# Attention and experts in one kernel: order of the read-back at a visit, places of key and factor products, second-weight splits in four parts

## The chip, the cores and the metric

The kernel runs on one core of one Trainium2 chip. The metric is the device time of one execution in microseconds (us); lower is better. In the texts PE is the matmul engine (TensorE), DVE is VectorE, ACT is ScalarE, POOL is GpSimd and SP is the engine whose queue issues most DMAs.

## What is computed

A polynomial-sketch attention over 4 batches, 4 heads, 1088 tokens and 32 columns a head, and behind it four experts, whose outputs are summed with normalized weights:

```python
def phi(x):
    a = np.einsum('rd,bhsd->bhsr', S1, x)
    b = np.einsum('rd,bhsd->bhsr', S2, x)
    return np.einsum('bhsi,bhsj->bhsij', a, b).reshape(*x.shape[:-1], r * r)
kv = np.einsum('bhsf,bhsd->bhfd', phi(k), v); z = np.sum(phi(k), axis=2)
attn = einsum(phi(q), kv) / (einsum(phi(q), z) + 1e-06)
x = attn.transpose(0, 2, 1, 3).reshape(4352, 128)
p = domain_probs / (domain_probs.sum(-1, keepdims=True) + 1e-09)
for e in range(4):
    out += p[:, e:e+1] * (np.maximum(x @ w1[e], 0.0) @ w2[e])
```

x has 4352 rows of 128; w1 is 128 x 1024 and w2 1024 x 128 for each of the four experts. All is float32.

## The kernel before, in words

**Chunks, experts, half-steps.** The 4352 rows of x are dealt into 11 chunks (`CHUNKS`, L95: 128, 448, 480, 480, six of 448, 128). A chunk m runs 16 steps: four for each expert e, and a step makes two blocks of 128 hidden rows, one in each half-step. "(m, e)" below is expert e of chunk m, and r0 to r7 are its eight half-steps. The half-steps are counted through the kernel; chunk m covers 32m to 32m+31. The lists `W2_AT` (L92), `KEYS_AT` (L814) and `UNITS_AT` (L820) give the half-steps at which side work is put into the stream: `first` (L1098) calls `work` once in each half-step, and `work` (L1408) runs what is due. `plan` entries (keys, units) are one higher than the count of `at_half` entries (w2 parts): 51 in `KEYS_AT` and 50 in `W2_AT` are the same half-step. Every engine executes its own instructions strictly in the order in which this program emits them.

**One half-step.** PE multiplies x by a block of w1 in three matmuls: two (L1147, L1148), then ACT scales the sum in PSUM (L1149), and one half-step later PE adds a third (L1199). ACT then takes the ReLU (L1203 for a block that is split, L1208 for one that is not). For a split block DVE makes the second part `hb` (L1175, in `lower`) and, once for two blocks, the third part `hd` (L1178). The second product (L1272, in `passed`) takes for a split block three matmuls, a, b and d, in PE's faster format (fp32r), and for a block that is not split one plain float32 matmul, "x", that is recorded as two. Six of eight blocks are split (`THREE`, L70); where (m, e) is in `MORE_IN` (L97), seven are. `DEAL` and `DEAL_MORE` (L75 to L83) say in which slot, counted in half-steps from r0, each second matmul is due: b1, which needs the second `hb`, at slot 4, x2 at slot 5, the last d6 and x7 at slot 11, which is r3 of the next expert. In chunk 1 the experts 0 and 1 are not split at all (`whole`).

**Accumulators.** PSUM has one bank `o0` (parts a and b) and one bank `o1` (parts d and x) for the second product. When an expert has ended, ACT copies `o0` (L1275) and DVE adds or copies `o1` out (L1304, L1301 in `gather`), POOL weights the result (L1311, L1313). The next expert's x2, or its d0 where there is no x2, cannot start before DVE has emptied `o1`.

**Attention and visits.** Attention runs beside the experts. Keys (`key_pieces`, L520) are turned, projected and multiplied: four `key_product` (L469, on DVE) for a batch. Queries come in units of 512 or 576 rows (`later`, L747). For a unit w: `unit_turn` transposes (DVE, L580), `unit_project` multiplies on PE, writes the factors to DRAM (L775), `unit_rows` (L779) reads them back as four tiles of factor rows (L786, L788, spread over 128 partitions), `unit_product` (L797) multiplies two pairs of them on DVE (L800), and the "visit" (L836) makes the attention output: PE multiplies, DVE divides (`attend_inverse`, `attend_scale`) and transposes. Then `attend_out` (L704), a generator, stores the tile to the DRAM buffer `xd` in four DMAs (L728) up to its first yield, and up to its second reads it back into `ring` in the layout of the experts (L739). At the end of the visit for w the factor rows of w+1 are read. All these DMAs are issued by SP, one after another. `token_parts` (L976) later splits a chunk of `ring` for the experts: ACT makes `xa` (L900), DVE `xb` and `xd` (L903), four steps ahead of the chunk.

**Second weights.** `second_weight_parts` (L918) splits the six blocks of w2[e] into three fp32r parts, in half-steps of chunk 1: ACT splits columns (L900), DVE joins (L903).

Of the kernel before, what the change touches and what calls it, by code (L numbers as in the profile page):

```python
# [24 lines left out]
def kernel(  # L25
# [65 lines left out]
    ]  # L91
    W2_AT = (36, 37, 38), (40, 41, 42), (44, 45, 46), (51, 52, 54)  # L92
    TOKENS_AT = 11, 12

    CHUNKS = [P, 448, 480, 480] + [448] * 6 + [P]  # L95
    NC = len(CHUNKS)
    MORE_IN = {(2, 2), (3, 2), (4, 2), (5, 1), (5, 2), (6, 2), (7, 0), (7, 1), (7, 2), (8, 0), (8, 1), (8, 2), (9, 0), (9, 1), (9, 2), (9, 3)}  # L97
    MORE_AT = {0: (100, 102), 1: (56, 57), 2: (38, 39), 3: (129, 131)}
    START = [sum(CHUNKS[:m]) for m in range(NC)]
    assert all(sum(u) == S for u in UNITS) and sum(CHUNKS) == B * S  # L100
# [79 lines left out]
    def more(m, e):  # L180
        return (m, e) in MORE_IN

# [361 lines left out]
    def key_sums(b):  # L544
        sums[b] = psum(ps_h, "h")
        for p in range(2):
            key_sum(b, p, sums[b])

    def key_end(b):

        key_blocks(b, sums.pop(b))
# [126 lines left out]
    def attend_inverse(nd, laid):  # L678

        tiles, banks = banks_of(laid)  # L680
        rc = apool.tile([P, XW // 32], F32, tag="rc", name="rc")
        for i, t0, t1 in banks:
            nc.vector.tensor_scalar(
                out=rc[:, H * t0 : H * t1],
                in0=_ap(nd[i], 0, P, D, [[D + 1, H * (t1 - t0)]]),
                scalar1=1e-6, scalar2=1.0, op0=ALU.add, op1=ALU.mult,
            )
        nc.vector.reciprocal(rc[:, 0 : H * tiles], rc[:, 0 : H * tiles])
        return rc

    def attend_scale(nd, laid, rc):

        xs = apool.tile([P, XW], F32, tag="qT", name="xs")
        banks = banks_of(laid)[1]
        for i, t0, t1 in banks:
            nc.vector.tensor_tensor(
                out=_ap(xs, 0, P, P * t0, [[D, H * (t1 - t0)], [1, D]]),
                in0=_ap(nd[i], 0, P, 0, [[D + 1, H * (t1 - t0)], [1, D]]),
                in1=_ap(rc, 0, P, H * t0, [[1, H * (t1 - t0)], [0, D]]),
                op=ALU.mult,  # L700
            )
        return xs
# [48 lines left out]
    def unit_turn(w):  # L751

        b, c, n, u = later[w]
        turned[w] = query_turn(b, c, n)
        if w and u == len(UNITS[b]) - 1 and b + 1 < B:
            load_rows(q, b + 1, "qn")

    def unit_project(w):

        b, c, n, u = later[w]  # L760
        qT, n2 = turned.pop(w), n // 2
        qc = psum(ps_h, "h")
        for i in range(2):
            for _ in range(2):
                on_side(
                    lambda s: qc[half[s], 0:n2],
                    lambda s: (sx if b else first_sx[0])[:, HP * i : HP * i + HP],
                    lambda s: qT[:, n2 * s : n2 * s + n2],
                    start=(i == 0),
                    stop=(i == 1),  # L770
                )
        qs = apool.tile([P, QW // 2], F32, tag="qf", name="qs")
        nc.scalar.copy(qs[:, 0:n2], qc[:, 0:n2])
        for s in range(2):
            nc.sync.dma_start(qd[b, u, :, n2 * s : n2 * s + n2], qs[half[s], 0:n2])  # L775
        if not w:
            load_rows(q, 1, "qn")
# [19 lines left out]
    def unit_product(w, p):  # L797

        n, (qp, qb) = later[w][2], factors[w]
        nc.vector.tensor_tensor(out=qp[p][:, 0:n], in0=qp[p][:, 0:n], in1=qb[p][:, 0:n], op=ALU.mult)  # L800

    def unit_visit(w):

        b, c, n, _ = later[w]
        products[w] = attend_products(b, c, n, factors.pop(w)[0])
# [3 lines left out]
    def add(hs, run):  # L809

        plan.setdefault(hs, []).append(run)

    FIRST_AT = (1, 2, 4, 5, 7, 9, 10, 12, 14, 15, 15, 15, 17, 18, 18, 19, 21, 23, 23)
    KEYS_AT = {  # L814
# [3 lines left out]
    }  # L818

    UNITS_AT = (  # L820
        (30, 43, 44, 47), (41, 73, 75, 79), (70, 103, 106, 111), (102, 134, 137, 143), (132, 157, 161, 175),
        (165, 191, 196, 207), (200, 214, 217, 222),
    )

    def lay_plan():

        of_first = queries(0, P, UNITS[0][1])
        for at in FIRST_AT:
            add(at, lambda: next(of_first, None))
        for w, (b, c, n, u) in enumerate(later):  # L830
            turn, p0, p1, at = UNITS_AT[w]
            add(turn, lambda w=w: unit_turn(w))
            for p, hs in enumerate((p0, p1)):
                add(hs, lambda w=w, p=p: unit_product(w, p))

            def visit(w=w, b=b, c=c, n=n, u=u):  # L836
                more = w + 1 < len(later)
                if w == 1:
                    key_sums(1)
                    key_end(1)  # L840
                    unit_project(w + 1)
                    unit_visit(w)
                else:
                    unit_visit(w)
                    if more:
                        unit_project(w + 1)
                    if 0 < b < B - 1 and u == len(UNITS[b]) - 1:
                        key_sums(b + 1)
                rc = attend_inverse(*products[w])
                out_of = attend_out(b, c, n, products[w][1], attend_scale(*products[w], rc))  # L850
                next(out_of)
                if more:
                    unit_rows(w + 1)
                next(out_of)

            add(at, visit)
        for b in range(1, B):
            key_pieces(b, *KEYS_AT[b])
            if b > 1:
                add(UNITS_AT[{2: 2, 3: 4}[b]][3], lambda b=b: key_end(b))  # L860

    def queries(b, c, n):
        qc = early.pop((b, c))
        qf = apool.tile([P, n], F32, tag="qf", name="qf")
        nc.vector.stream_shuffle(in_=qc[:, 0:n], out=qf[:, 0:n], mask=mask_lo)
        yield
        nc.vector.tensor_tensor(out=qf[:, 0:n], in0=qc[:, 0:n], in1=qf[:, 0:n], op=ALU.add)
        yield
        qb = apool.tile([P, QW], F32, tag="qb", name="qb")
        nc.vector.stream_shuffle(in_=qf[:, 0:n], out=qb[:, 0:n], mask=mask_b)  # L870
        yield
        qp = query_tiles()
        for x in range(2):
            qa = apool.tile([P, QW], F32, tag="qa", name="qa")
            nc.vector.stream_shuffle(in_=qf[:, 0:n], out=qa[:, 0:n], mask=mask_a[x])  # L875
            yield
            for p in range(2):
                query_product(qp, p, x, n, qa, qb)
                yield
        weight_part("b", 0, 0)  # L880
        yield
        yield
        yield
        yield from attend(b, c, n, qp)
# [14 lines left out]
    def split(a, w, scale):  # L899
        nc.scalar.activation(a, w, ACTF.Copy, scale=scale * NEAR)  # L900

    def join(out, in0, scale, in1, op):
        nc.vector.scalar_tensor_tensor(out=out, in0=in0, scalar=scale, in1=in1, op0=ALU.mult, op1=op)  # L903
# [14 lines left out]
    def second_weight_parts(e):  # L918


        w, n = w2_of[e, 0], N3 * DM
        vab = cpool.tile([P, F], F32R, tag=f"w1_{e}", name="vab")
        vb = cpool.tile([P, 2 * n - F], F32R, tag=f"vb_{e}", name="vb")
        a, lows = vab[:, 0:n], [(0, F - n, vab[:, n:F]), (F - n, n, vb[:, :])]
        for c, z, b in lows:
            split(a[:, c:z], w[:, c:z], 4096.0)
            join(b, w[:, c:z], 4096.0, a[:, c:z].bitcast(F32), ALU.subtract)
            yield
        split(a, w, 1.0)
        d = cpool.tile([P, n], F32R, tag=f"w2_{e}0", name="vd")[:, :]  # L930
        for c, z, b in lows:
            join(d[:, c:z], b.bitcast(F32), 1.0, a[:, c:z].bitcast(F32), ALU.subtract)
        w2_parts[e] = {
            THREE[i]: tuple(
                x[:, DM * i - c : DM * i - c + DM] for x, c in ((a, 0), next((x, c) for c, z, x in lows if DM * i < z), (d, 0))
            )
            for i in range(N3)
        }
        yield
# [393 lines left out]
    def at_step(step, *calls):  # L1333
        to_part.setdefault(step, []).extend(calls)
# [4 lines left out]
    for what, e, h, step in SPLITS:  # L1339
        at_step(step, lambda p=(what, e, h): weight_part(*p))  # L1340
    for e, at in zip((2, 3, 0, 1), W2_AT):
        parts_of = second_weight_parts(e)
        for hs in at:
            at_half.setdefault(hs, []).append(next_of(parts_of))
# [135 lines left out]
```

## Time and profile before

| what | value |
|---|---|
| runs | 451.64, 450.03, 450.16 us; median 450.16 |
| the profiled execution | 450.71 us, its span from first to last instruction 448.9 us |
| granted PE clock | 1.000 over the span |
| busy: DVE, ACT, POOL | 381.4, 335.1, 136.2 us |
| first matmuls L1147, L1148, L1199 | 288 each, 129.1, 106.1 and 107.1 us busy |
| DVE L1175 and L1178 | 220 of 625 ns mean, 118 of 1111 ns mean |
| DVE key product L473 | 576 columns, 0.71 to 1.16 us |
| DVE factor product L800 | 14, 670 to 752 ns |
| SP: factor rows | 14 of L786, 526 to 912 ns to issue each |
| DMA queues | 38.46 MB in 51155 packets, mean 86 GB/s |

The profile is of one execution; its times count from its first instruction. A matmul's recorded length is modelled and longer than its step: two fp32r matmuls of 448 columns start 0.20 us apart and are recorded as 0.37 us each. Steps from start to start are therefore used for PE, DVE and ACT. "[1.73 <-DMA ring<-xd]" behind a line of the timeline says that the engine stood idle for 1.73 us before it, and what ended the wait. SPq lines are the issue of DMAs, not their transfer; the trace also holds the packets of the transfers, with start, length and size.

### The profile page before, as it was taken

The numbers are of one execution on the slowest core, as the hardware profiler recorded it, in microseconds if no ns is written. First come the engines' busy times: TensorE is split into PE (matmuls) and PEld (weight loads), VectorE is DVE, ScalarE is ACT, GpSimd is POOL, SyncE is SP. The second block draws the span as 40 slices with busy tenths as digits, with TensorE's granted clock in tenths as the row PEclk, the third lists the DMA queues.
The fourth block names the chain that finished last, engine by engine and source line by source line (L and its number), as shares of the span: only waits on it lengthen the run. The fifth ranks groups of instructions, "written<-read, shape, count | busy, mean of one in ns | idle before, by whom it ended". The sixth has DMA issues, their size and how long they took to land.

```text
span 448.9 us, 8582 instructions
## 1 busy us (share of the span) xinstructions
PE 440.0 (98%) x2989; PEld 370.6 (83%) x2989; DVE 381.4 (85%) x629; ACT 335.1 (75%) x711; POOL 136.2 (30%) x219
## 2 busy tenths in 40 slices
PE   9999998999999999999999989999999999999997
PEld 6887677778887888888888878888888888888886
DVE  5998888888999789889986888899988898898853
ACT  4478887857878588868885688687888888888831
POOL 7359233211143023213331333133323413331440
PEclk9999999999999999999999999999999999999999
DMA  7866275134702341135022710351301030017501
GB/s 192 267 182 172 69 191 105 35 82 117 164 22 46 93 118 22 60 92 141 22 42 45 155 31 23 78 142 45 66 21 20 23 62 22 20 36 190 187 1 28
DMA packets 51155, 38.46 MB, mean 86 GB/s; under 512 B 24968, under 2 KB 45384, under 8 KB 51112
## 3 DMA queue, kind: packets, MB, share of 16 engines
q1 hardware_dynamic: 49672, 36.79, 32.5%
q0 software_dynamic: 1216, 1.06, 1.0%
q8 instruction: 23, 0.38, 0.3%
q14 instruction: 20, 0.16, 0.1%
q10 hardware_dynamic: 224, 0.07, 0.1%
HBM read 32.68 MB, written 5.21 MB: 84 GB/s over the span
## 4 chain that ended last, share of the span: by engine, by line
PE 89%; DMA 5%; DVE 3%; issue 1%; SPq 0%; ACT 0%; DVEq 0%; ACTq 0%
PE o L1272 37%; PE h L1199 13%; PE h L1147 12%; PE h L1148 12%; PE h L262 8%; DMA ring<-xd 4%; PE o L262 3%; PE o L1253 3%; PE h L457 1%; DMA kn<-in_k_dram 1%; DVE qp L593 0%; DVE hd L1178 0%; DVE qa L875 0%; PE h L1117 0%; ACT h L1149 0%
## 5 line engine op out<-in xcount | busy, mean ns | idle before, releaser
L1149 ACT ACTIVATE h<-h 128x448 f32<-128x448 f32 (+1 forms) x288 | 155.2, 539 | 69.2 <-PE h L1148 63.3
L1175 DVE SCALAR_TENSOR_TENSOR hb<-h,ha 128x448 fp32r<-128x448 f32 (+1 forms) x220 | 134.9, 625 | 25.8 <-ACT ha L1203 22.8
L1178 DVE SCALAR_TENSOR_TENSOR hd<-ha,hb 128x896 fp32r<-128x896 f32 (+3 forms) x118 | 131.1, 1111 | 13.8 <-PE o L1272 4.2
L1147 PE MATMUL h<-xa,wa 128*128 128x448 f32 (+1 forms) x288 | 129.1, 448 | 0.0
L1203 ACT ACTIVATE ha<-h 128x448 fp32r<-128x448 f32 (+1 forms) x220 | 120.5, 548 | 0.0
L1311 POOL TENSOR_TENSOR ev<-ev,gate 128x256 f32<-128x256 f32 (+2 forms) x54 | 48.6, 900 | 218.9 <-DVE ev L1304 208.8
L1199 PE MATMUL h<-xd,wd 128*128 128x448 f32 (+1 forms) x288 | 107.1, 372 | 3.8 <-ACT h L1149 3.8
L1148 PE MATMUL h<-xb,wb 128*128 128x448 f32 (+1 forms) x288 | 106.1, 368 | 0.0
L1272 PE MATMUL o<-ha,vab 128*128 128x448 f32 (+1 forms) x204 | 75.9, 372 | 0.0
L1147 PEld LDWEIGHTS h<-xa,wa 128*128 128x128 f32 x288 | 54.2, 188 | 16.7 <-issue 11.7
L1148 PEld LDWEIGHTS h<-xb,wb 128*128 128x128 f32 x288 | 54.2, 188 | 16.6 <-issue 12.2
L1199 PEld LDWEIGHTS h<-xd,wd 128*128 128x128 f32 x288 | 54.0, 188 | 12.4 <-ACT h L1149 6.2
L1272 PE MATMUL o<-hd,vd 128*128 128x448 f32 (+1 forms) x204 | 61.7, 372 | 0.0
L1272 PE MATMUL o<-hb,vb 128*128 128x448 f32 (+1 forms) x136 | 50.2, 369 | 0.1
L1313 POOL TENSOR_TENSOR total<-total,ev 128x256 f32<-128x256 f32 (+2 forms) x54 | 47.9, 887 | 4.2
L1272 PE MATMUL o<-hid,w_sb 128*128 128x448 f32 (+1 forms) x104 | 48.5, 547 | 0.4 <-DVE ev L1304 0.3
L1272 PEld LDWEIGHTS o<-hd,vd 128*128 128x128 f32 x204 | 37.9, 188 | 4.4 <-issue 0.8
L1272 PEld LDWEIGHTS o<-ha,vab 128*128 128x128 f32 x204 | 38.3, 188 | 3.8
L1208 ACT ACTIVATE hid<-h 128x448 f32<-128x448 f32 (+1 forms) x68 | 37.4, 550 | 1.0 <-PE h L1199 0.8
L1311 POOL TENSOR_TENSOR total<-ev,gate 128x256 f32<-128x256 f32 (+2 forms) x18 | 12.3, 707 | 60.0 <-issue 43.0
L1272 PEld LDWEIGHTS o<-hb,vb 128*128 128x128 f32 x136 | 25.5, 188 | 2.8 <-DVE hb L1175 0.5
L1272 PE MATMUL o<-hb,vab 128*128 128x448 f32 (+1 forms) x68 | 25.0, 368 | 0.0
(156 smaller groups left out, 460.8 us busy)
## 6 DMA issues: line engine op xcount, KB each, us to landing
gate<-gates SPq DMA_DIRECT2D x22, 224.0 KB
kn<-in_k_dram SPq DMA_DIRECT2D x4, 544.0 KB
vn<-in_v_dram SPq DMA_DIRECT2D x16, 128.0 KB
qp<-qd SPq DMA_DIRECT2D x8, 256.0 KB
w_last<-in_moe_w_dram SPq DMA_DIRECT2D x4, 512.0 KB
qp<-qd SPq DMA_DIRECT2D x6, 288.0 KB
qb<-qd SPq DMA_DIRECT2D x6, 288.0 KB
w_sb<-in_moe_w_dram SPq DMA_DIRECT2D x3, 512.0 KB
```

The source lines that it names most:

```text
L262: nc.tensor.matmul(out(s), weights(s), moving(s), **flags)
L1147: nc.tensor.matmul(g, wa[:, e, w], xa, start=True, stop=False)
L1148: nc.tensor.matmul(g, wb[:, e, w], xb, start=False, stop=True)
L1149: nc.scalar.activation(g, g, ACTF.Copy, scale=1.0 + R12)
L1175: nc.vector.scalar_tensor_tensor(out=hb, in0=g, scalar=0.0, in1=high, op0=ALU.max, op1=ALU.subtract)
L1178: nc.vector.scalar_tensor_tensor(out=d2, in0=a2.bitcast(F32), scalar=R12, in1=b2.bitcast(F32), op0=ALU.mult, op1=ALU.subtract)
L1199: nc.tensor.matmul(g, w, x, start=False, stop=True, skip_group_check=True)
L1203: nc.scalar.activation(ha, g, ACTF.Relu, scale=NEAR)
L1208: nc.scalar.activation(hid[i][j], g, ACTF.Relu)
L1272: nc.tensor.matmul(acc[m, e][o][:, 0:n], w, h, start=first_one, stop=last)
L1311: nc.gpsimd.tensor_tensor(out=to[:, x], in0=ev[:, x], in1=g[:, x], op=ALU.mult)
L1313: nc.gpsimd.tensor_tensor(out=total[m][:, x], in0=total[m][:, x], in1=ev[:, x], op=ALU.add)
```

## The change

```diff
-    W2_AT = (36, 37, 38), (40, 41, 42), (44, 45, 46), (51, 52, 54)
+    W2_AT = (36, 37, 38, 39), (40, 41, 42, 43), (44, 45, 46, 46), (50, 51, 53, 54)
...
-    MORE_IN = {(2, 2), (3, 2), (4, 2), (5, 1), (5, 2), (6, 2), (7, 0), (7, 1), (7, 2), (8, 0), (8, 1), (8, 2), (9, 0), (9, 1), (9, 2), (9, 3)}
+    MORE_IN = {(2, 2), (3, 2), (4, 2), (5, 2), (6, 2), (7, 0), (7, 1), (7, 2), (8, 0), (8, 1), (8, 2), (9, 0), (9, 1), (9, 2), (9, 3)}
...
     KEYS_AT = {
-        1: ((36, 37, 38), (38, 39, 40), (39, 40, 41), (56, 62, 66, 70)),
+        1: ((36, 37, 38), (38, 39, 40), (39, 40, 41), (51, 54, 60, 66)),
         2: ((79, 79, 79), (83, 84, 85), (84, 85, 86), (90, 93, 97, 100)),
-        3: ((111, 111, 111), (115, 116, 117), (116, 117, 118), (122, 127, 148, 153)),
+        3: ((111, 111, 111), (115, 116, 117), (116, 117, 118), (122, 127, 148, 169)),
     }
     UNITS_AT = (
-        (30, 43, 44, 47), (41, 73, 75, 79), (70, 103, 106, 111), (102, 134, 137, 143), (132, 157, 161, 175),
-        (165, 191, 196, 207), (200, 214, 217, 222),
+        (30, 43, 44, 47), (41, 71, 77, 79), (68, 103, 106, 111), (102, 134, 137, 143), (132, 161, 171, 175),
+        (172, 191, 196, 207), (200, 217, 219, 223),
     )
...
                 next(out_of)
+                next(out_of)
                 if more:
                     unit_rows(w + 1)
-                next(out_of)
...
-        split(a, w, 1.0)
+        for c, z, b in lows:
+            split(a[:, c:z], w[:, c:z], 1.0)
+            if c == 0:
+                yield
```

- At a visit the read of x from `xd` into `ring` is issued ahead of the four reads of factor rows, not behind them.
- The last split of a second weight, one ACT instruction of 768 columns, becomes one of 256 and one of 512, and a fourth entry in `W2_AT` says where the last part goes. The parts of expert 1 start at 50 instead of 51.
- Of batch 1, the four key products go from 56, 62, 66 and 70 to 51, 54, 60 and 66. Of batch 3 the last goes from 153 to 169.
- A unit's entry in `UNITS_AT` is (turn, first product, second product, visit). Unit 1's products go from 73 and 75 to 71 and 77; unit 2's turn from 70 to 68; unit 4's products from 157 and 161 to 161 and 171; unit 5's turn from 165 to 172; unit 6's products from 214 and 217 to 217 and 219, its visit from 222 to 223.
- (5, 1) is taken out of `MORE_IN`: seven split blocks become six there, and one block goes as a plain float32 matmul.

## Prediction

> **What bounds the kernel now.** I read first the busy times, then the waits, then the timeline around each wait of PE.
>
> ```profile
> PE 440.0 (98%) x2989; PEld 370.6 (83%) x2989; DVE 381.4 (85%) x629; ACT 335.1 (75%) x711; POOL 136.2 (30%) x219
> ```
>
> PE is busy for 440.0 of 448.9 us at a granted clock of 1.000. So only two things can move the time: PE's work, and the moments in which PE stands. I listed all steps from one PE start to the next and took off the usual step of the same pair (0.20 us for fp32r with 448 columns, 0.75 us for a plain float32 product). What is left over is small in number. The waits name the two largest:
>
> ```profile
> ACT xa L900 <- DMA ring<-xd: 3.9, 2, 2.1
> ...
> PE h L1199 <- ACT h L1149: 3.8, 3, 2.0
> ```
>
> ACT waited twice for the read-back of x, 3.9 us in all, and PE three times for ACT, 3.8 us. That these are the same events, the timeline shows:
>
> ```profile
> 68.47 0.37 PE L1148 MATMUL h<-xb,wb 128*128 128x448 f32 x1
> 69.36 0.60 ACT L900 ACTIVATE xa<-ring 128x480 fp32r<-128x480 f32 x1 [1.73 <-DMA ring<-xd]
> ...
> 69.86 0.53 ACT L1149 ACTIVATE h<-h 128x448 f32<-128x448 f32 x1
> ...
> 70.44 0.47 PE L1199 MATMUL h<-xd,wd 128*128 128x448 f32 x1 [1.60 <-ACT h L1149]
> ```
>
> `xa` stands in ACT's order ahead of the scaling that PE needs; x is not there; PE's step is 1.97 us instead of 0.20. The same at the read for chunk 6:
>
> ```profile
> 258.37 0.58 ACT L900 ACTIVATE xa<-ring 128x448 fp32r<-128x448 f32 x1 [2.14 <-DMA ring<-xd]
> ...
> 259.43 0.47 PE L1199 MATMUL h<-xd,wd 128*128 128x448 f32 x1 [2.00 <-ACT h L1149]
> ```
>
> There the step is 2.36. Why x is late, SP's queue tells:
>
> ```profile
> 245.38 1.79 SPq L728 DMA_DIRECT2D xd<-y  x4
> 247.34 0.56 SPq L786 DMA_DIRECT2D qp<-qd  x1
> ...
> 249.80 0.97 SPq L739 DMA_DIRECT2D ring<-xd  x2
> ```
>
> Stores, then four factor reads, then x. In the packets of the trace the four reads (1152 KB) run from 248.69 to 257.18, and the last of x ends at 260.2. At the earlier visit the rows run from 58.79 to 66.74 and the 240 KB of x end at 68.09.
>
> The other stands of PE, each with the slower step behind it (0.31 instead of 0.20, so 0.1 more): 65.31, 0.37, for ACT, which had the 768-column split (0.74 us) in front; 89.48, 0.24, for DVE's `hb`, behind a turn and a key product in one half-step; 96.13, 0.51, and 216.30, 0.18, for `o1`:
>
> ```profile
> 94.76 0.75 DVE L800 TENSOR_TENSOR qp<-qp,qb 128x576 f32<-128x576 f32 x1
> ...
> 95.43 0.65 DVE L1304 TENSOR_TENSOR ev<-ev,o 128x480 f32<-128x480 f32 x1
> ...
> 96.13 1.07 PE L1272 MATMUL o<-hid,w_sb 128*128 128x480 f32 x2 [0.35 <-DVE ev L1304]
> ```
>
> A product ahead of the emptying of `o1`, and x2 waits.
>
> **The change part by part.**
>
> *The read of x goes first.* It now waits on SP for the stores to land. That wait is shown where no factor rows follow: the last visit's stores are issued until 313.29, the read of its last part at 314.51, so 1.2 us. Then 0.9 to 1.4 us to issue, 1.3 us to the first packet (57.45 to 58.79), and about 2 us for 240 to 288 KB at the 145 KB/us of the factor rows. At the first visit x then lands near 62.5, needed at 67.6; at the other near 252, needed at 256.2. Both waits go. ACT's next scaling starts 0.5 us after `xa`, near 68.1 in place of 69.86, and PE asks for it at 68.68: nothing is late next. Gain 1.87 and 2.27, with the step behind each. What pays is the queue behind: factor rows (2.1 to 2.6 us later), key, value and gate loads (1 us). Rows that ended at 66.74, 162.25, 209.35 and 257.18 are multiplied from 91.7, 186.5, 217.2 and 266.1 on, unit 4 even later than now. Only unit 6 is near: rows until 298.31, products at 297.40 and 300.99. Its rows come to end near 301.5, and its products move to about 301.0 (first pair, landed by 298.5) and 304. I price this at 0; without that cover, rival 4.
>
> *Second weights.* ACT's 768 columns (step 0.73) become 256 (0.32) and 512 (0.52): 0.11 more each, four times. Experts 2, 3 and 0 have them in half-steps in which PE needs 1.36 us and ACT 0.88 besides, so 0. For expert 1, at 65.31, 0.52 stands in front of ACT instead of 0.73, and PE comes later by what follows next: 0.1 to 0.2 stay, gain 0.27.
>
> *Key products of batch 1, and unit 1.* Turn (68), key product (66) and factor product (71) stand in half-steps of their own: the `hb` of 88.78 comes 1.2 us sooner, gain 0.34. Unit 1's second product goes behind the emptying of `o1`: gain 0.61. But the first two key products go where chunk 1 has its own emptying:
>
> ```profile
> 60.07 0.43 DVE L903 SCALAR_TENSOR_TENSOR vab<-w_sb,vab 128x256 fp32r<-128x256 f32 x1
> ...
> 60.41 0.62 DVE L1301 COPY ev<-o 128x448 f32<-128x448 f32 x1
> ...
> 61.75 0.92 PE L1272 MATMUL o<-hid,w_sb 128*128 128x448 f32 x2
> ```
>
> In the changed program's order DVE has after `vab` the key product (step 0.67, from 67.63), then `vb` (0.57), then this copy. It starts at 60.41 + 0.67 + 0.57 = 61.65 and ends at 62.27; PE's x2 wants `o1` at 61.75. **A new stand of 0.55**, 0.65 with the step behind it, at (1, 2). Bounds: 0, if DVE gets to `vab` earlier, and 1.0.
>
> *Batch 3, units 4 to 6, (5, 1).* Before 216.30 a key product (0.67) goes from DVE's order: gain 0.29. It, unit 4's second product and unit 5's turn now stand in (5, 1): transpose at 231.59 (0.56), `hb`, key product, `hb`, `hd`, product, then the emptying. From 232.15: 0.67 more to the second `hb` (233.35, after 0.38 idle there now), `hd` 234.08, product 235.1, emptying 235.7 to 236.25. With six split blocks x2 is due there near 236.5. It fits by 0.2; by the case at 96.13, the same order, it would miss by 0.6. I take 0.1. Leaving `MORE_IN` costs PE a plain product (0.75) for three fp32r (0.61): 0.13, and takes 1.2 us from DVE. Unit 6: the emptying, 304.38 now, comes at 305.0 to 305.6, x2 at 306.4: 0.
>
> **Sum.** Gains 1.87 + 2.27 + 0.27 + 0.34 + 0.61 + 0.29 = 5.65. Costs 0.65 + 0.13 + 0.1 = 0.88. Net 4.8. The profiled execution took 450.71 (span 448.9, 1.8 around it): 445.9. The median of the runs is 0.55 below it: **445.4 us**.
>
> **The rivals.**
>
> 1. *DVE becomes the bound at more places.* The emptying of `o1` misses x2 at (5, 1) and at (6, 3) by 0.62 each, as at 96.13, and DVE is slowed by POOL: the key product at 76.68, beside a POOL add, took 1.16 us instead of 0.75, and the late copy puts POOL's four operations beside the second key product. For it: DVE without idle time from 209 to 219 and from 295 to 308 (9.65 of 10.0 and 12.60 of 13.0 us busy). Against: the 0.2 to 0.9 us left by the sums above. 445.4 + 0.52 + 0.62 + 0.4 = 446.9. The Trainium skill, "SBUF — State Buffer", section "Who interferes with whom", says that a VectorE instruction with two SBUF inputs and a GpSimd instruction that reads SBUF shut each other out for their whole length; the 1.16 agrees, and by that rule the 0.4 is the rule and not the exception.
>
> 2. *One of the two reads is still late.* For: a read of x took 7 to 10 us from issue to last packet. Against: that was behind 1152 KB, which now come after it. 445.4 + 2.1 = 447.5.
>
> 3. *The read goes first in the queue and lands no sooner*, because the wait for the stores and the loads of keys beside it take as long as the rows did. The order itself is certain: the built program has x ahead of the rows at every such visit. Both waits stay: 445.4 + 4.1 = 449.5.
>
> 4. *Slower: SP stands for the stores and the factor rows of unit 6 are late.* DVE takes its products in order; each us that the rows land behind 304 is a us on DVE, then on PE. Place: (6, 3). It starts to cost when the wait for the stores is over 3.5 us instead of 1.2, and the kernel is slower than now by 0.5% once it is 4.8 + 2.3 + 3.5, near 10 us: 453. For: the change does hold SP. Against: 1.2 us is the only such wait in the trace.
>
> **How the numbers follow.** Forecast 0.68, rival 1 0.14, rival 2 0.07, rival 3 0.05, rival 4 0.04, anything else 0.02. 0.5% is 2.25 us, about what a measurement of this kernel can tell from no change. Faster by more: the forecast, rival 1 and most of rival 2, 0.88; same: rival 3 and the rest of 2, 0.07; slower: 0.05. The range: all gains with the copy in time and 0.4 of smaller stands gives 444.3; rivals 1 and 2 are taken in up to 447.6.
>
> **What would show it.** In the profile after: no wait "ACT xa L900 <- DMA ring<-xd"; SP issues L739 about 1.2 us after L728; PE's steps at both places 0.2 us. A new wait of x2 for the copy of `o` in (1, 2), about 0.5 us. No wait for `ev` in (2, 1) and (4, 3), little or none in (5, 1) and (6, 3). Wrong if unit 6's products wait for DMA, or if DVE shows new waits of over 0.5 us in more than one expert.

## The result and the profile after

The changed kernel takes 448.17 us (median; 447.42 to 451.23), the kernel before, run beside it, 450.79 (449.45 to 454.75). The ratio is 0.9941, 95% interval [0.9922, 0.9960]. The forecast was 445.4 us, in a range of 444.3 to 447.6, and a gain of 4.8; measured is a gain of 2.6, and the time lies above the range. Of the 2.8 us between 448.17 and 445.4, 0.6 is the base: the forecast counted from 450.16, the median of three runs of before, and the median of 22 is 450.79. The other 2.2 are gain that did not come. The profiled execution took 448.23 us with a span of 446.5, against 448.9 before, at a granted clock of 1.000 in both.

In this part and all that follow, lines of the changed kernel from L1069 on are three higher than those of before: L1175 is L1178, L1199 is L1202, L1301 is L1304; ring_first_only and five_one_only keep the lines of before. First the busy times on the page of after.

```profile
PE 440.3 (99%) x2988; PEld 370.7 (83%) x2988; DVE 380.5 (85%) x627; ACT 335.0 (75%) x715; POOL 135.5 (30%) x219
```

PE has one matmul less and ACT four instructions more, as the diff says. PE is busy for as long as before; what shrank is the time in which it stands. The waits of PE in after (who waits for whom: us in total, times, longest):

```profile
PE h L1202 <- ACT h L1152: 1.2, 1, 1.2
...
PE o L1275 <- DVE ev L1304: 0.4, 1, 0.4
```

Before, PE waited three times and 3.8 us for ACT; now once, 1.2 us. Both waits for x are gone: ACT's `xa` starts without a wait at the two places of the prediction, here in the timeline of after.

```profile
69.77 0.61 ACT L900 ACTIVATE xa<-ring 128x480 fp32r<-128x480 f32 x1
...
255.79 0.58 ACT L900 ACTIVATE xa<-ring 128x448 fp32r<-128x448 f32 x1
```

But the one wait for ACT that is left is not one of the three. It is new, at 46.01, and no step of the prediction named it. The timeline of after leads back from it:

```profile
41.38 0.63 ACT L900 ACTIVATE vab<-w_sb 128x512 fp32r<-128x512 f32 x1
...
42.05 0.43 DVE L903 SCALAR_TENSOR_TENSOR vd<-vab 128x256 fp32r<-128x256 f32 x1 [2.21 <-ACT vab L900]
...
42.39 0.68 DVE L903 SCALAR_TENSOR_TENSOR vd<-vb,vab 128x512 fp32r<-128x512 f32 x1
...
42.99 0.42 DVE L467 TENSOR_TENSOR fs<-h,fs 128x256 f32<-128x256 f32 x1
...
43.33 1.75 DVE L903 SCALAR_TENSOR_TENSOR wb<-w_sb,wa 128x512 fp32r<-128x512 f32 x2
...
43.89 1.66 POOL L423 COPY vx<-vn 128x512 f32<-128x512 f32 x2
44.43 0.37 PE L1151 MATMUL h<-xb,wb 128*128 128x448 f32 x1
45.11 0.42 ACT L900 ACTIVATE vab<-w_sb 128x256 fp32r<-128x256 f32 x1 [1.97 <-DVE wb L903]
45.43 0.53 ACT L1152 ACTIVATE h<-h 128x448 f32<-128x448 f32 x1
...
46.01 0.47 PE L1202 MATMUL h<-xd,wd 128*128 128x448 f32 x1 [1.22 <-ACT h L1152]
```

Read it from below. PE stands for the scaling L1152. That stands in ACT's order behind `vab`, the first split of expert 3, which waits 1.97 us for DVE's `wb`: `vab` is written over the first-weight tile that `wb` reads. `wb` is late since it stands in DVE's order behind both `vd`, the joins of expert 2, and DVE was idle for 2.21 us in front of those until ACT's 512-column split of 41.38 was through. This split is the half-step that the change put between the two parts of the last split. The timeline of before has no such gap:

```profile
39.12 0.84 ACT L900 ACTIVATE vab<-w_sb 128x768 fp32r<-128x768 f32 x1
39.99 0.42 DVE L903 SCALAR_TENSOR_TENSOR vd<-vab 128x256 fp32r<-128x256 f32 x1 [0.46 <-ACT vab L900]
...
41.60 1.28 DVE L903 SCALAR_TENSOR_TENSOR wb<-w_sb,wa 128x512 fp32r<-128x512 f32 x2
42.92 0.42 ACT L900 ACTIVATE vab<-w_sb 128x256 fp32r<-128x256 f32 x1
```

One split, the joins 0.46 us behind it, `wb` 1.7 us sooner, and expert 3's `vab` waits for it for less than 0.1 us. PE's step, 0.20 us there, is 1.58 us in after.

The second new stand is the one the prediction did name, at (1, 2). Timeline of after:

```profile
61.86 0.42 DVE L903 SCALAR_TENSOR_TENSOR vab<-w_sb,vab 128x256 fp32r<-128x256 f32 x1
...
62.20 0.75 DVE L473 TENSOR_TENSOR kp<-fs 128x576 f32<-128x576 f32 x1
...
62.87 0.68 DVE L903 SCALAR_TENSOR_TENSOR vb<-w_sb,vab 128x512 fp32r<-128x512 f32 x1
...
63.47 0.62 DVE L1304 COPY ev<-o 128x448 f32<-128x448 f32 x1
...
64.14 1.02 PE L1275 MATMUL o<-hid,w_sb 128*128 128x448 f32 x2 [0.42 <-DVE ev L1304]
```

The key product and `vb` stand ahead of the copy of `o1`; PE's step is 0.59 over the usual.

### The profile page after: what moved, and what is told of

It is laid out like the page before. It is cut to its first block, busy times and chain, and to the rows that moved or that the text cites. A ratio compares the mean times of both kernels' runs of the same rounds, so it can differ in the third digit from the quotient of the medians.

```text
span 446.5 us, 8575 instructions
## 1 busy us (share of the span) xinstructions
PE 440.3 (99%) x2988; PEld 370.7 (83%) x2988; DVE 380.5 (85%) x627; ACT 335.0 (75%) x715; POOL 135.5 (30%) x219
## 4 chain that ended last, share of the span: by engine, by line
PE 96%; DVE 2%; DMA 1%; ACT 1%; issue 1%; SPq 0%
PE o L1275 40%; PE h L1202 13%; PE h L1150 13%; PE h L1151 13%; PE h L262 9%; PE o L262 3%; PE o L1256 2%; PE h L457 1%; DMA kn<-in_k_dram 1%; DVE wb L903 0%; ACT h L1152 0%; PE h L1120 0%; DVE kp L473 0%; DVE vd L903 0%; DVE hb L1178 0%
## 5 line engine op out<-in xcount | busy, mean ns | idle before, releaser
L1152 ACT ACTIVATE h<-h 128x448 f32<-128x448 f32 (+1 forms) x288 | 155.4, 540 | 69.2 <-PE h L1151 63.2
L1178 DVE SCALAR_TENSOR_TENSOR hb<-h,ha 128x448 fp32r<-128x448 f32 (+1 forms) x219 | 133.9, 623 | 28.6 <-ACT ha L1206 25.7
L1314 POOL TENSOR_TENSOR ev<-ev,gate 128x256 f32<-128x256 f32 (+2 forms) x54 | 49.5, 917 | 216.2 <-DVE ev L1307 203.9
L1202 PE MATMUL h<-xd,wd 128*128 128x448 f32 (+1 forms) x288 | 107.2, 372 | 1.2 <-ACT h L1152 1.2
L1202 PEld LDWEIGHTS h<-xd,wd 128*128 128x128 f32 x288 | 54.0, 188 | 10.1 <-ACT h L1152 3.7
L1316 POOL TENSOR_TENSOR total<-total,ev 128x256 f32<-128x256 f32 (+2 forms) x54 | 45.8, 848 | 4.2
```

The lines of the kernel that those rows point to most:

```text
L1152: nc.scalar.activation(g, g, ACTF.Copy, scale=1.0 + R12)
L1178: nc.vector.scalar_tensor_tensor(out=hb, in0=g, scalar=0.0, in1=high, op0=ALU.max, op1=ALU.subtract)
L1202: nc.tensor.matmul(g, w, x, start=False, stop=True, skip_group_check=True)
L1314: nc.gpsimd.tensor_tensor(out=to[:, x], in0=ev[:, x], in1=g[:, x], op=ALU.mult)
L1316: nc.gpsimd.tensor_tensor(out=total[m][:, x], in0=total[m][:, x], in1=ev[:, x], op=ALU.add)
```

## The experiments

Theory: the change loses 1.5 us at 44 to the half-step inside expert 2's last split, through DVE's queue; the rest of the ledger holds. Rivals: the later factor rows cost something; the moved products crowd DVE; POOL's copies slow DVE; the reads of x bring less than booked. All kernels were timed beside before on the same chip; rows with different figures in the third column are of different sessions, so compare them by the ratio. "Extra step" is PE's step from one start to the next, less the usual step of that pair, in the profiled execution; "at 44" gives the time at which that step starts.

| kernel | median us (range) | beside before | ratio [95%] |
|---|---|---|---|
| after | 448.17 (447.42-451.23) | 450.79 | 0.9941 [0.9922, 0.9960] |
| ring_first_only | 447.63 (446.90-447.95) | 450.59 | 0.9925 [0.9899, 0.9951] |
| w2_parts_only | 451.74 (449.43-454.38) | 450.59 | 1.0022 [0.9993, 1.0050] |
| w2_as_before | 446.98 (446.33-447.31) | 450.59 | 0.9913 [0.9885, 0.9941] |
| w2_third_and_fourth_together | 446.48 (446.32-446.56) | 450.59 | 0.9902 [0.9871, 0.9933] |
| moves_only | 447.25 (446.95-447.76) | 450.24 | 0.9935 [0.9911, 0.9958] |
| x_behind_rows | 449.60 (447.74-452.72) | 450.24 | 0.9989 [0.9965, 1.0012] |
| keys_behind_copy | 446.82 (446.29-447.12) | 450.24 | 0.9921 [0.9894, 0.9947] |
| five_one_seven_split | 448.85 (447.79-450.76) | 450.24 | 0.9973 [0.9953, 0.9994] |
| five_one_only | 449.11 (447.66-451.53) | 450.54 | 0.9977 [0.9955, 0.9999] |
| ring_first_unit_six | 446.84 (446.55-447.58) | 450.54 | 0.9924 [0.9900, 0.9947] |
| w2_expert_two_only | 446.89 (446.33-447.28) | 450.54 | 0.9922 [0.9899, 0.9945] |
| w2_expert_one_later | 446.72 (446.06-446.81) | 450.54 | 0.9916 [0.9893, 0.9939] |
| after_no_value_copy | 447.52 (447.31-449.44) | 451.16 | 0.9930 [0.9906, 0.9954] |
| before_no_value_copy | 449.75 (448.30-451.12) | 451.16 | 0.9967 [0.9942, 0.9992] |

### Each part alone, and the change without one part

**w2_third_and_fourth_together**: after, but the two parts of the last split in one half-step, so as many instructions as after.

```diff
-    W2_AT = (36, 37, 38, 39), (40, 41, 42, 43), (44, 45, 46, 46), (50, 51, 53, 54)
+    W2_AT = (36, 37, 38, 38), (40, 41, 42, 42), (44, 45, 46, 46), (50, 51, 53, 54)
```

> The changed kernel, but for experts 2 and 3 the two halves of the last split are put in the same half-step (36, 37, 38, 38 and 40, 41, 42, 42). The number of instructions stays. Theory A: what costs is the half-step between the halves, with DVE's join behind the second, not the extra instruction; the stand near 44 us goes, 1.2 to 1.5 us faster than the changed kernel. Theory C (the extra ACT instruction costs): same as the changed kernel within 0.3 us.

446.48 us, the lowest of all kernels here. No extra step at 44; that at (1, 2), 0.59, stays. So it is not the cost of four more ACT instructions but the half-step between them.

**w2_as_before**: after, with the splits and their places as in before.

```diff
-    W2_AT = (36, 37, 38, 39), (40, 41, 42, 43), (44, 45, 46, 46), (50, 51, 53, 54)
+    W2_AT = (36, 37, 38), (40, 41, 42), (44, 45, 46), (51, 52, 54)
...
-        for c, z, b in lows:
-            split(a[:, c:z], w[:, c:z], 1.0)
-            if c == 0:
-                yield
+        split(a, w, 1.0)
```

> The changed kernel with the second-weight splits and their places as before. Theory A: the stand near 44 us is gone, 1.2 to 1.5 us faster than the changed kernel, so 3.8 to 4.2 us faster than before. Without the earlier split of expert 1 DVE reaches the copy of o1 in (1, 2) later or sooner by one join: order key product, first join, copy, so the copy ends near 61.7 in the clock of before and x2 hardly waits, which would give 0.5 more. Theory B: same time as the changed kernel.

446.98. The stand at 44 is gone, and that at (1, 2) too: with expert 1's parts one half-step later `vb` is behind the copy, and the key product alone does not make it late. In its place stand 0.36 at 65.0 and 0.28 at 69.1.

**w2_parts_only**: before with the new splits and places, all else as before.

```diff
-    W2_AT = (36, 37, 38), (40, 41, 42), (44, 45, 46), (51, 52, 54)
+    W2_AT = (36, 37, 38, 39), (40, 41, 42, 43), (44, 45, 46, 46), (50, 51, 53, 54)
...
-        split(a, w, 1.0)
+        for c, z, b in lows:
+            split(a[:, c:z], w[:, c:z], 1.0)
+            if c == 0:
+                yield
```

> The kernel before with only the second-weight splits in four parts and their new places. Theory A: DVE stands for the second half of the last split of expert 2 and holds the first-weight parts behind it, ACT then stands for those; PE loses 1.4 to 1.6 us near 44 us, gains 0.2 at 65 us; 1.2 to 1.4 us slower than before, ratio 1.003. Theory B: within 0.3 us of before; the wait near 44 us in the profile after was a chance of that execution.

451.74, slower than before by 0.22% [-0.07%, 0.50%]; the interval includes no change. The profile has an extra step of 0.92 at 44 and one of 0.62 at 51.6. It also has a stand of 2.06 for x at 69.8, and behind that something the prediction had not allowed for; see the last section.

**ring_first_only**: before with the read of x ahead of the factor rows.

```diff
                 next(out_of)
+                next(out_of)
                 if more:
                     unit_rows(w + 1)
-                next(out_of)
```

> The kernel before with one thing changed: x is read back ahead of the factor rows. Theory A (the reads give all that the prediction said, and the time is lost again at the second weights): both waits of ACT for the read go, 4.1 us faster than before, ratio 0.991. Theory B (the read gives less, because SP's wait for the stores and the traffic beside it take a part back): 1 to 3 us faster, and a wait for the read or for factor rows is seen.

447.63. Both waits for x are gone, 4.1 us by the profile before, but 3.0 are gained. Two new stands of PE, 0.94 at 295.1 and 0.61 at 297.2, say why; timeline of ring_first_only:

```profile
294.96 0.69 DVE L800 TENSOR_TENSOR qp<-qp,qb 128x512 f32<-128x512 f32 x1 [2.04 <-DMA qb<-qd]
295.57 0.62 DVE L1175 SCALAR_TENSOR_TENSOR hb<-h,ha 128x448 fp32r<-128x448 f32 x1
...
296.24 0.47 PE L1272 MATMUL o<-hb,vb 128*128 128x448 f32 x1 [0.77 <-DVE hb L1175]
```

DVE waits 2.04 us for unit 6's factor rows, `hb` stands behind it, and PE waits for `hb`. This is the place and the mechanism of rival 4.

**ring_first_unit_six**: the same, with unit 6 where the change has it.

```diff
-        (165, 191, 196, 207), (200, 214, 217, 222),
+        (165, 191, 196, 207), (200, 217, 219, 223),
```

> Before with x read first, and unit 6's products and visit at 217, 219, 223 in place of 214, 217, 222. Theory A (ring_first_only lost 1.55 us at 295 to 298 because DVE waited for unit 6's factor rows; the later products are the cover): those two steps of PE are back to the usual 0.20, and the gain is the two waits, 1.87 + 2.27 = 4.1: 446.2 (446.0 to 446.5). Theory B (the rows only hide another want of DVE there): steps of over 0.4 us remain between 294 and 306, 447 and more.

446.84. The two stands are gone (0.13 is left at 301.5). So the moved products are the cover that the prediction named. The time is 0.3 over the top of the expected 446.0 to 446.5: the profiled execution, 447.34, has an extra step of 0.75 at 46.9, in code that is the same as before's. after_no_value_copy and before_no_value_copy deal with it.

**moves_only**: before with the new `MORE_IN`, `KEYS_AT` and `UNITS_AT`; x still behind the rows, splits as before.

```diff
-    MORE_IN = {(2, 2), (3, 2), (4, 2), (5, 1), (5, 2), (6, 2), ...
+    MORE_IN = {(2, 2), (3, 2), (4, 2), (5, 2), (6, 2), ...
...
-        1: (..., (56, 62, 66, 70)),
+        1: (..., (51, 54, 60, 66)),
...
-        3: (..., (122, 127, 148, 153)),
+        3: (..., (122, 127, 148, 169)),
...
-        (30, 43, 44, 47), (41, 73, 75, 79), (70, 103, 106, 111), (102, 134, 137, 143), (132, 157, 161, 175),
-        (165, 191, 196, 207), (200, 214, 217, 222),
+        (30, 43, 44, 47), (41, 71, 77, 79), (68, 103, 106, 111), (102, 134, 137, 143), (132, 161, 171, 175),
+        (172, 191, 196, 207), (200, 217, 219, 223),
```

> The kernel before with only the places of key and factor products, turns and the visit, and (5, 1) with six split blocks. Theory A: the stands at 89.5, 96.1 and 216.3 us go (1.2 us), (5, 1) costs 0.13; the copy of o1 in (1, 2) has one key product ahead of it but the join vb behind it, ends near 61.7 where x2 is due at 61.75, so 0 to 0.2; both waits for the read of x stay. 0.8 to 1.1 us faster than before, ratio 0.998. Theory B (the moves make new waits of DVE at (5, 1) and (6, 3)): no gain or slower.

447.25: 3.0 us gained where about 1 was expected. The wait for x at 257 is gone although x is still read last. The key is what stands in front of the visit of unit 4 in DVE's order. Timeline of before:

```profile
237.79 1.19 DVE L1175 SCALAR_TENSOR_TENSOR hb<-h,ha 128x448 fp32r<-128x448 f32 x2
242.29 1.09 DVE L1178 SCALAR_TENSOR_TENSOR hd<-ha,hb 128x896 fp32r<-128x896 f32 x1 [3.32 <-PE o L1272]
...
244.65 0.71 DVE L709 STREAM_TRANSPOSE y<-xs 128x512 f32<-128x512 f32 x1
```

`hd` waits 3.32 us for PE, and the transpose `y`, from which x is stored, comes behind it.

**five_one_only**: before, only (5, 1) out of `MORE_IN`.

```diff
-    MORE_IN = {(2, 2), (3, 2), (4, 2), (5, 1), (5, 2), (6, 2), ...
+    MORE_IN = {(2, 2), (3, 2), (4, 2), (5, 2), (6, 2), ...
```

> Before with one edit: (5, 1) leaves MORE_IN; x is still read behind the factor rows. Theory A (the second wait for x hangs on DVE's order: with seven split blocks the hd of 242.29, which waits 3.32 us for PE, stands ahead of the visit of unit 4; with six it stands behind it): the transpose y comes near 240 in place of 244.65, x lands 3 to 5 us sooner, the wait of 2.27 at 257 is gone, PE's work is 0.13 more, so 448.1 against 450.3, ratio 0.995. The first wait for x (1.9 us) stays. Theory B (only the read order takes that wait away, and moves_only lost it by its other moves): 450.4, wait still there.

Its timeline at the same place:

```profile
236.98 1.09 DVE L1178 SCALAR_TENSOR_TENSOR hd<-ha,hb 128x896 fp32r<-128x896 f32 x1
237.99 0.62 DVE L1175 SCALAR_TENSOR_TENSOR hb<-h,ha 128x448 fp32r<-128x448 f32 x1
...
239.94 0.71 DVE L709 STREAM_TRANSPOSE y<-xs 128x512 f32<-128x512 f32 x1
```

`hd` is made for two split blocks at once. With six blocks no pair stands there whose `hd` has to wait for PE, `y` comes 4.71 us sooner (about 1 of it because this execution is ahead of before's by then), and at 255.20 ACT's `xa` has its x without a wait. So one wait for x had two remedies in this change. The median, 449.11, is 1.0 above the expectation, the runs reach 451.5, and the profiled execution, 447.66, is the lowest of its runs: it has an extra step of 0.94 at 47.0 and behind that no wait for x at 68.7 either, because PE comes later. The three longest runs, 450.62 to 451.53, are the three with a granted clock of 0.996; the last section says what that is.

**x_behind_rows**: after with the old order of the reads.

```diff
                 next(out_of)
-                next(out_of)
                 if more:
                     unit_rows(w + 1)
+                next(out_of)
```

> The changed kernel with x read back behind the factor rows again. Theory A: the wait for the read of chunk 2 and that of chunk 6 come back, unless DVE's earlier visit in (5, 1), where no third part stands in front of it now, brings the stores of unit 4 forward by 2 us or more: then only the first comes back. 1.9 to 4.1 us slower than the changed kernel. Theory B: under 1.5 us slower.

449.60. The profiled execution (span 446.0) has no wait for x at either place: at 257 thanks to (5, 1), at 68 because the stands at 44.2 (1.33) and 63.1 (0.60) make PE late. Of the read order's gain in after, this execution shows nothing; the medians show 1.4 us, and the runs here spread to 452.7. That x is late in the longer ones is likely, but not shown: there is no trace of a longer run. Two of the twelve (450.90 and 452.72) have a granted clock of 0.996.

**five_one_seven_split**: after with (5, 1) back in `MORE_IN`.

```diff
-    MORE_IN = {(2, 2), (3, 2), (4, 2), (5, 2), (6, 2), ...
+    MORE_IN = {(2, 2), (3, 2), (4, 2), (5, 1), (5, 2), (6, 2), ...
```

> The changed kernel with (5, 1) back at seven split blocks. By the sum: PE has 0.13 us less work there; DVE has one more part (0.55) and a third part (0.6) in an expert that holds a key product, a factor product, a turn and a visit. If DVE has no room there, a new wait of PE of 0.3 to 1 us; if it has, 0.1 us faster than the changed kernel.

448.85, a new stand of 0.40 at 239.5, and the stand at 44 is 2.17 us in this execution. The ratios of this kernel and of after overlap, so what the edit is worth behind the moved read is not settled; the 0.40 is in its profile.

**keys_behind_copy**: w2_as_before with the key products of batch 1 behind the copy.

```diff
-        1: (..., (51, 54, 60, 66)),
+        1: (..., (53, 55, 60, 66)),
```

> The changed kernel with the second weights as before and the first two key products of batch 1 at 53 and 55 instead of 51 and 54, behind the copy of o1. Theory A: x2 in (1, 2) no longer waits; against the changed kernel 1.4 us for the second weights and 0.7 us for the copy, 2.0 to 2.2 us faster, 4.6 to 4.9 us faster than before, ratio 0.9895. Theory B: the key products are late somewhere else, and nothing is gained over the second weights alone.

446.82, the same as w2_as_before within the intervals: x2 at (1, 2) is in time in both, and products placed later crowd 68.6 and 69.9 (0.39 and 0.28). Its profiled execution also has 0.79 at 46.9, where POOL's copy makes a DVE join late (see after_no_value_copy and before_no_value_copy).

### How many experts matter, and what POOL has to do with it

**w2_expert_two_only**: after with 38, 38 for expert 2 alone.

```diff
-    W2_AT = (36, 37, 38, 39), (40, 41, 42, 43), (44, 45, 46, 46), (50, 51, 53, 54)
+    W2_AT = (36, 37, 38, 38), (40, 41, 42, 43), (44, 45, 46, 46), (50, 51, 53, 54)
```

> After with expert 2's last two splits in one half-step again (38, 38), all else as after, so expert 3's stay apart (42, 43). Theory A (the stand at 44.4 comes from expert 2's joins alone, which hold back the first-weight parts of DVE and with them the tile that expert 3's first split writes): no step over 0.3 at 44, 446.5 as with both experts together. Theory B (expert 3 and expert 0, priced at nothing too, cost their share): a stand of 0.4 to 1.4 us between 45 and 53, 447 to 448.

446.89. Nothing at 44, but 1.07 at 50.5, so both theories hold in part: expert 2 makes the stand at 44, and expert 3's own half-step costs too. Timeline:

```profile
49.21 1.84 POOL L1314 TENSOR_TENSOR total<-ev,gate 128x256 f32<-128x256 f32 x2 [3.23 <-DVE ev L1304]
49.37 1.23 DVE L903 SCALAR_TENSOR_TENSOR vd<-vb,vab 128x512 fp32r<-128x512 f32 x1
...
50.52 1.07 DVE L800 TENSOR_TENSOR qp<-qp,qb 128x512 f32<-128x512 f32 x1
```

Expert 3's `vd` comes so late that it runs beside POOL's additions, 1.23 us in place of 0.68; PE waits for the factor product behind it. In after the same two DVE instructions take 1.22 and 1.09 us, but behind the stand at 44 PE comes late enough not to wait for them; w2_parts_only, with 0.92 at 44, has the 0.62 at 51.6 from the same pair.

**w2_expert_one_later**: third and fourth together, and expert 1's first two parts one half-step later.

```diff
-    W2_AT = (36, 37, 38, 39), (40, 41, 42, 43), (44, 45, 46, 46), (50, 51, 53, 54)
+    W2_AT = (36, 37, 38, 38), (40, 41, 42, 42), (44, 45, 46, 46), (51, 52, 53, 54)
```

> After with the last two splits of experts 2 and 3 in one half-step (38, 38 and 42, 42), and expert 1's first two one half-step later (51, 52 in place of 50, 51), so that vb stands behind the copy of o1 in DVE's order. Theory A (x2 at (1, 2) waits because the key product and vb stand ahead of that copy): the step of 0.59 us at 61.5 is gone, 0.15 to 0.4 stays near 65, 445.9 (445.7 to 446.2). Theory B (the key product ahead of the copy is enough): the stand stays with 0.3 or more, 446.3 to 446.6.

446.72, not faster than w2_third_and_fourth_together (446.48). The 0.59 at (1, 2) is gone, so `vb` ahead of the copy is what makes it late, but 0.27 and 0.29 stand at 66.7 and 69.4, and 0.44 at 46.9.

**after_no_value_copy** and **before_no_value_copy**: POOL's copy of batch 1's values is left out, so batch 1 is computed with old values.

```diff
     def value_copy(b):
-        copy = nc.gpsimd.tensor_copy if b == 1 else nc.scalar.copy
+        if b == 1:
+            return
+        copy = nc.scalar.copy
```

> After without POOL's copy of batch 1's values into vx (three instructions at 43.9 to 45.8; batch 1 is then computed with old values). Theory A (the stand at 44.4 is the queue behind DVE's late joins, made longer by POOL: the second wb there took 1.15 us beside the copy, 0.63 otherwise): wb is 0.63 to 0.69, PE's extra step at 44 falls from 1.38 to about 0.85, 447.6 against 448.2. Theory B (the queue alone): 1.4 stays, 448.2. Theory C (POOL's copy is the whole cause): no step over 0.3, 446.7.

447.52 (the intervals of this ratio and of after's overlap), and 0.91 for 1.38 at 44. Timeline (lines two higher than in after):

```profile
42.93 1.28 DVE L905 SCALAR_TENSOR_TENSOR wb<-w_sb,wa 128x512 fp32r<-128x512 f32 x2
...
44.25 0.42 ACT L902 ACTIVATE vab<-w_sb 128x256 fp32r<-128x256 f32 x1 [1.50 <-DVE wb L905]
```

The two `wb` take 1.28 us together, as in before; in after they took 1.75. So of the 1.38 us, 0.9 is the queue behind the late joins, and 0.5 is POOL's copy, into which the lateness pushed the second `wb`. Other profiles agree: where the half-step is there and the copy comes behind `wb`, the extra step is 0.92 (w2_parts_only); where the copy meets `wb`, it is 1.33, 1.38 and 2.17 (x_behind_rows, after, five_one_seven_split).

> Before without POOL's copy of batch 1's values. Theory A (in seven of the thirteen kernels with profiles a DVE instruction of expert 3's split ran 1.2 to 1.8 us beside that copy, 0.43 otherwise, and PE then stood for 0.4 to 0.9 us near 47; before's profiled execution missed it by under 0.1 us, so that others of its executions have it): vab near 43.4 takes 0.43, no step over 0.3 near 47, the median is 0.3 to 0.6 below before's, 450.0 against 450.4. Theory B (POOL's copy costs nothing here): no difference, 450.4.

449.75 against 451.16: the first theory's direction, more than its 0.3 to 0.6. How much of it is the copy itself is not settled: ten of the 21 runs of before beside it have a granted clock of 0.996 or less (the last section says what that is), and two of the twelve here; the medians of the others are 450.39 and 449.66, 0.7 apart. `vab` near 43.4 takes 0.42 and PE has no extra step near 47. What the copy does otherwise, the timeline of five_one_only shows:

```profile
43.56 1.76 DVE L903 SCALAR_TENSOR_TENSOR vab<-w_sb,vab 128x256 fp32r<-128x256 f32 x1 [0.48 <-ACT vab L900]
43.85 1.19 POOL L423 COPY vx<-vn 128x512 f32<-128x512 f32 x2
...
46.81 0.85 ACT L900 ACTIVATE vab<-w_sb 128x768 fp32r<-128x768 f32 x1 [0.97 <-DVE vb L903]
...
48.15 0.47 PE L1199 MATMUL h<-xd,wd 128*128 128x448 f32 x1 [0.77 <-ACT h L1149]
```

POOL's copy starts 0.29 us into DVE's `vab`, which alone takes 0.43, and `vab` ends only behind both copies. In before the copy started at 43.78 and `vab` ran from 43.37 to 43.80. Of the fourteen profiles in which the copy is made, `vab` was hit in six (1.18 to 1.84 us) and `wb` in three; in five the copy came too late to hit either, and `vb` behind them took 0.82 to 1.43 us in place of 0.68.

## Why the prediction was wrong where it was, point by point

PE's landmarks of after against before, step by step, in the profiled executions (positive is later):

| stretch | predicted us | measured us |
|---|---|---|
| start of chunk 1 (no code differs) | 0 | +0.34 |
| expert 2's split, 44 to 46 | 0 | +1.46 |
| (1, 2), copy of `o1` | +0.65 | +0.69 |
| expert 1's split | -0.27 | -0.22 |
| first read of x | -1.87 | -1.84 |
| batch 1's keys, unit 1 | -0.95 | -0.94 |
| batch 3's key product, 216 (measured with +0.14 at 140, not forecast) | -0.29 | -0.15 |
| (5, 1) | +0.23 | +0.34 |
| second read of x | -2.27 | -2.26 |
| rest | 0 | +0.10 |
| sum | -4.77 | -2.48 |

The first row is chance: the code up to there is the same in both kernels, and the two executions differ by 0.34 us at its end.

**The step that failed** is in *Second weights*: "Experts 2, 3 and 0 have them in half-steps in which PE needs 1.36 us and ACT 0.88 besides, so 0." The sum for ACT was right; ACT had the room. The term put at 0 measured 1.46 us. What the step left out is the engine behind ACT. Two joins of DVE wait for the later part, three more instructions of DVE stand behind them, and the last of those frees the tile that ACT's next split writes. A half-step of delay on one engine came back to it through two queues, for about 0.9 us, and made `wb` late enough to meet POOL's copy, for another 0.5. The runs with the parts together in one half-step, or with the old split, have neither. Expert 3's half-step, also put at 0, costs 1.07 where expert 2's does not come first (w2_expert_two_only). DVE's idle time, not ACT's, was the thing to look up: before, DVE came to `vd` 0.46 us ahead of ACT, and ACT already stood idle for 0.09 us in front of `vab` until `wb` was done, so there was no room at all. The signs that the prediction named for itself at the two reads and at (1, 2) were all seen, and unit 6's products did not wait for DMA; none of its signs was a place near 44. Of the signs against it, new waits of DVE came (2.21 at 42.0 for ACT, and 1.72 at 243.6 where before has 3.32 at 242.29), and only the first cost PE more than 0.1 us.

**The reads of x go first**: both waits gone, as forecast. That x landed at 62.7 where 62.5 was forecast is luck: the new stand at 44 had made the stores 1.7 us later than in before, and in ring_first_only, without that stand, x landed at 60.9. The forecast was too cautious by 1.6. It added the time to issue the read to the time until its first packet, but the first packet came 1.0 us after the start of the issue (58.65 to 59.61), and the packets took 1.3 us in place of 2. At the second visit x landed at 246.9 where 252 was forecast: too cautious by 3.8 even with (5, 1) as before (248.2 in ring_first_only), and the visit itself came 4.3 us sooner through (5, 1) (`y` at 240.35, not 244.65). The prediction had booked the whole 2.27 on the read order and priced (5, 1) at its own instructions only. five_one_only and moves_only lose the wait with the old order. The sum was not harmed, since either remedy suffices. Nor are the gains independent: each stand ahead of 68 shortens the first wait by its own length (0.86 of about 1.8 is left in moves_only behind stands of 0.57, 0.09 and 0.18, none in x_behind_rows). The prediction's reading that the last of x came at 260.2 in before is wrong: `xa` starts on that x at 258.37. No term of the sum hangs on it.

**SP's wait for the stores**, 1.2 us by the prediction, is 1.47 at the first visit in after (57.20 + 1.78 to 60.45). At the later visits the first part of x is read 0.1 us behind the stores and the next part 1.4 us behind them. So it was in the trace of before from which the 1.2 was taken: 314.51 is the second read there, the first was issued at 313.46. **The cover of unit 6** was sized as it is: without the moved products the rows are late and cost 0.94 + 0.61 (ring_first_only), with them 0.13 (ring_first_unit_six) or nothing (after). Rival 4's mechanism is real; without the cover it costs 1.5 us, less than the reads of x gain.

**Key products and (1, 2)**: right in place and size, 0.59 against 0.55 for the stand. **Rival 1** did not come at (5, 1) and (6, 3), where DVE was in time. POOL slowing DVE, which it held for 0.4 us of a possible loss, came at `wb` (0.5 us) and not at the second key product.

**What remains open**: which stand makes single runs of after reach 451.2, and what x does in the longer runs of x_behind_rows; there is no trace of such a run. A part is on record: the four longest of after's 22 runs (450.15 to 451.23) are the four with a granted clock of 0.996, the other 18 (447.42 to 448.95) have 0.999 or 1.000. One stretch of half clock, described in the last section, takes 0.004 off the mean of such a run. The longest stand in profiles of after's code is the one at 44 (1.33 to 2.17 us); that it was the cause is not shown.

## What to carry to other kernels

When a side job gets one more step, follow its consumer: who joins the parts, what stands behind that join in its engine's order, and whose buffer the last of these frees; an engine with room in each half-step can still be held up by its own delay. Where two edits can each end the same wait, book the gain once, and expect a wait to shrink by whatever new stand comes ahead of it.

## What the runs showed of the hardware that was not expected

**A stand of 2 us can cost 3.7.** In w2_parts_only PE stood 2.06 us too long at 69.8 for x. The views by stretch (columns: length; busy time and instructions of PE, PEld, DVE, ACT, POOL; granted clock; DMA share; GB/s), w2_parts_only first and before second:

```profile
68.00:72.00 4.00, 2.21 (x11) 1.69 (x9) 2.94 (x5) 1.97 (x5) 0.00 (x0) 1.00 1.00 174
72.00:76.00 4.00, 3.90 (x10) 2.87 (x11) 3.21 (x5) 2.52 (x7) 0.73 (x1) 0.61 0.59 115
```

```profile
68.00:72.00 4.00, 2.40 (x11) 1.57 (x10) 2.58 (x5) 2.65 (x6) 0.00 (x0) 1.00 0.84 150
72.00:76.00 4.00, 4.00 (x20) 3.38 (x19) 3.30 (x6) 2.63 (x7) 2.53 (x4) 1.00 0.24 60
```

Just behind the stand the granted clock is 0.61 on the mean of 4 us, PE starts 10 matmuls in place of 20, its step is 0.37 us in place of 0.20, and the steps there add up to 1.6 us more than the same steps of before. before_no_value_copy shows the same behind 2.03 us (clock 0.59, again 1.6 us). Stands of 1.76 and 2.16 us (before) and 2.17 (five_one_seven_split) were not followed by it, so length alone does not decide.

The clock records of the traces show what decides here. The half clock (granted 0.50) lasts from 72.87 to 76.28 in w2_parts_only and from 71.87 to 75.29 in before_no_value_copy, 3.41 us both times; the full clock ahead of it lasts 68.27 us and behind it 375.47, 20 and 110 times as long. So the clock changes on a grid of 3.41 us, and the grid starts at another time in each execution. In the one stretch of the grid ahead of the half clock PE was idle, by its recorded lengths, for 1.90 and 1.86 us. The stands of 2.16 and 2.17 us were cut by the grid into 1.33 and 0.67 us of idle time each, and the one of 1.76 us, 1.60 idle, lay within one stretch. In all fifteen profiles that have clock records, every stretch at full clock with 1.86 us or more of idle PE, those at the kernel's end included, is followed by half clock, and none with 1.68 us or less; what lies between is not known. The Trainium skill, "TensorE: Matmul & The Clock Gate", section "What's actually happening", says that the clock falls to half after an idle window of about 3.4 us, and that this window runs free. The 3.41 us and the changing start agree; but here the window was idle for little more than half of its length. A wait near 2 us is thus worth up to 1.8 times its length in executions in which it falls into one stretch, and a ledger made from an execution without it books too little.

**DVE waits out a POOL copy to its end.** A join of 0.43 us took 1.76 when POOL's copy began during it. The Trainium skill, "SBUF — State Buffer", section "Who interferes with whom", says that a VectorE instruction with two SBUF inputs contends with a GpSimd instruction that reads SBUF, and that the one issued first decides. The first half agrees. The second does not agree with `vab` of five_one_only by the recorded starts, 43.56 for DVE and 43.85 for POOL: there the later one went through first. POOL's recorded spans are rough, so this is no proof against it.
